# Attention and MLP side by side: projecting the first 512 rows before they are normalised, with dummy products in the opening and new planner thresholds

## The chip, the cores and the metric

The kernel runs on one core of one Trainium2 chip. The metric is the device time of one execution in microseconds (us). TensorE is called PE, VectorE DVE, ScalarE ACT, GpSimd POOL and SyncE SP. A *tile* of x is 128 rows of 640 values; PSUM has eight banks.

## The reference, cut to what matters

S = 2048 rows, D = 640, 32 heads of 20 with one shared key and value head, F = 1536, all bf16.

```python
xn = (x - mean(x)) / sqrt(var(x) + 1e-5)          # per row
q = (xn @ wq) -> 32 heads; k = xn @ wk; v = xn @ wv
p = softmax(q @ k.T * 20 ** -0.5)                 # per head
attn = concat_heads(p @ v) @ wo
h = relu(xn @ w1 + b1) ** 2
return x + attn + (h @ w2 + b2)
```

## The kernel before, in words

**A planner orders everything.** The Python code holds a list scheduler (`Sched`). Streams (generators) ask for pieces of work with `Req(engine, duration, latency, instructions, dependencies, priority)`, and `Until` holds a stream back. When the kernel is built, the planner picks piece after piece with durations written in the code, and so fixes one static instruction order for each engine. On the chip every engine runs its list in order and waits on semaphores for what its pieces depend on. Landing times of DMAs are also figures in the code (`xland`, `TLAND`, `XRL`). If one of them is too short, the chip's engine simply waits at that place of its list.

**Attention.** Queries lie in 4 blocks of 512 rows, times 8 groups of 4 heads: 32 blocks `b` (`NBLK`; block 0 is heads 0 to 3, block 1 heads 4 to 7). Keys come in 16 tiles. A *unit* is one head, one key tile and 512 queries: one score product `ps<-qT,kT` (L1154) into a PSUM bank. There are 2,048 units. 1,468 go to ACT, which takes two or three at once (L1334, 1,024 or 1,536 columns, into a ring `PT`). 580 go to DVE, which makes an approximate exponential from integer arithmetic (L1431 from PSUM into `pbx`, then L1452 and on POOL L1514 for three shifted copies). Value products are L1621. Thresholds that decide how the planner shares the units and when it gives up banks are in `PLAN`, one row for each half block, 64 rows of 13 figures.

**The rest** is put between the units: query projections (`u_QT`, `u_QP`), the MLP's first product (`u_FFN`, L939 on DVE, squares on POOL L947), and the output products (L783). Norms and packed heads travel by small DMAs on SP's queue.

**The opening.** SP loads x in five DMAs (tiles 0-1, 2-3, 4-7, 8-11, 12-15; row `st*128 + p` on partition p) with wq between the third and the fourth; ACT's queue loads wk and wv. `x_sb` lies in `pbx`, normalised tiles `xn_sb` in `big`. Per tile: statistics (`stats`, L683 and L686 on DVE; tile 2 on ACT, L673 and L675), then `rst` (L694 LN and L698 exponential on ACT, one for four tiles), then `xnorm` (L712 on DVE; tile 3 on ACT, L714). Tiles 0 to 4 are transposed by PE (L772) and copied out (L727 on ACT, L726 on DVE); tiles 5 to 15 by transposing DMAs on SP (L732). `u_K0` and `u_Q0` project the first 512 rows, in halves of 256, with `wk_c` and `wq_sb`; the mean key of the first tile is subtracted from all keys (`nk0`, L816, L817, L821). `u_V` makes values (L842, L846, then POOL L850 and L854). `S_PRO` starts these streams for tiles 0 to 3. Key tiles 4 to 7 (`u_KT`, copy at L807) need tiles 4 to 7 transposed.

**Dummy products.** `warmup` (L650) gives PE 20 products of 512 columns on constants. `S_FILL` adds fill products when PE's planned load in the last 1,500 ns is under `PE_FILL`: L1551 before the first value product (4 x 512 columns), L1550 with zeros afterwards.

## Time and profile before

| | |
|---|---|
| median of 3 runs | 702.17 us (701.01 to 703.31) |
| profiled execution | 702.17 us, span 700.0 us |
| mean granted PE clock | 0.995 |
| busy PE / DVE / ACT / POOL | 684.3 / 659.3 / 680.5 / 411.8 us |
| ACT exponentials (L1334) | 672.1 us in 684 instructions |
| first exponential starts | 14.31 us |
| last exponential ends | 691.56 us |

The span runs from the first to the last instruction; the 2.17 us beside it lie outside. Busy PE is modelled and overlaps, so 98% is not PE at its peak. The opening up to 14 us, the exponentials, and 8 us of output products, additions and stores at the end follow one another.

### The profile page before, as it was taken

The numbers are of one execution on the slowest core, as the hardware profiler recorded it, in microseconds if no ns is written. First come the engines' busy times: TensorE is split into PE (matmuls) and PEld (weight loads), VectorE is DVE, ScalarE is ACT, GpSimd is POOL, SyncE is SP. The second block draws the span as 40 slices with busy tenths as digits, with TensorE's granted clock in tenths as the row PEclk, the third lists the DMA queues.
The fourth block names the chain that finished last, engine by engine and source line by source line (L and its number), as shares of the span: only waits on it lengthen the run. The fifth ranks groups of instructions, "written<-read, shape, count | busy, mean of one in ns | idle before, by whom it ended". The sixth has DMA issues, their size and how long they took to land.

```text
span 700.0 us, 23262 instructions
## 1 busy us (share of the span) xinstructions
PE 684.3 (98%) x9837; PEld 218.7 (31%) x9837; DVE 659.3 (94%) x1135; ACT 680.5 (97%) x705; POOL 411.8 (59%) x678
## 2 busy tenths in 40 slices
PE   8899999999999999999999999999999999999997
PEld 4232222222223333332223333333223333333333
DVE  6788999999999999999999999999999999999994
ACT  6799999999999999999999999999999999999995
POOL 2245576767675656667766666666666656656510
PEclk9899999999999999999999999999999999999999
DMA  6433233101110111210110111111110011121001
GB/s 201 67 74 120 54 109 85 27 20 27 29 20 13 39 26 39 50 36 19 24 25 18 45 27 39 32 30 41 28 26 19 15 38 47 27 50 32 11 3 40
DMA packets 37330, 29.30 MB, mean 42 GB/s; under 512 B 19594, under 2 KB 32875, under 8 KB 37227
## 3 DMA queue, kind: packets, MB, share of 16 engines
q1 hardware_dynamic: 35915, 27.76, 16.6%
q8 instruction: 79, 1.29, 0.8%
q10 hardware_dynamic: 1312, 0.05, 0.1%
q14 instruction: 24, 0.20, 0.1%
HBM read 10.87 MB, written 2.62 MB: 19 GB/s over the span
## 4 chain that ended last, share of the span: by engine, by line
ACT 76%; PE 13%; DVE 10%; DMA 1%; issue 0%; POOL 0%; DVEq 0%; POOLq 0%
ACT PT L1334 75%; DVE pbx L1431 5%; PE ps L783 4%; PE ps L1621 4%; PE ps L1154 4%; DVE pbx L1452 3%; PE ps L650 1%; DVE hT_tmp L939 1%; DMA xnT<-big 1%; DVE stats L683 0%; DVE Tn L1666 0%; DVE big L712 0%; ACT xnT L727 0%; DVE qpk L894 0%; PE ps L1551 0%
## 5 line engine op out<-in xcount | busy, mean ns | idle before, releaser
L1334 ACT ACTIVATE PT<-ps 128x1024 bf16<-128x1024 f32 (+1 forms) x684 | 672.1, 1138 | 5.3 <-PE ps L1154 5.0
L1514 POOL TENSOR_SCALAR pbx<-pbx 128x576 int16<-128x576 uint16 (+17 forms) x508 | 309.5, 629 | 185.6 <-DVE pbx L1452 173.8
L1431 DVE TENSOR_SCALAR pbx<-ps 128x512 int16<-128x512 f32 (+1 forms) x568 | 377.2, 689 | 16.6 <-PE ps L1154 15.3
L1154 PE MATMUL ps<-qT,kT 20*128 20x512 bf16 x2048 | 267.9, 385 | 3.8 <-ACT PT L1334 1.9
L1452 DVE TENSOR_SCALAR pbx<-pbx 128x2048 int16<-128x2048 int16 x305 | 209.2, 705 | 0.8
L1621 PE MATMUL ps<-pbx,vp 128*32 128x512 bf16 x1740 | 161.4, 384 | 1.1 <-DVE pbx L1452 0.8
L1154 PEld LDWEIGHTS ps<-qT,kT 20*128 20x128 bf16 x2048 | 66.9, 91 | 260.6 <-ACT PT L1334 183.3
L1621 PE MATMUL ps<-PT,vx 128*32 128x512 bf16 x1468 | 142.2, 384 | 1.8 <-ACT PT L1334 1.8
L783 PE MATMUL ps<-w_sb,big 128*32 128x320 bf16 x1536 | 80.7, 302 | 0.1
L783 PE MATMUL ps<-xnT,w_sb 128*32 128x512 bf16 x960 | 77.3, 384 | 0.4 <-DVE pbx L1431 0.2
L947 POOL TENSOR_TENSOR big<-hT_tmp 128x224 bf16<-128x224 bf16 (+4 forms) x85 | 55.8, 668 | 32.5 <-DVE pbx L1452 32.5
L1621 PEld LDWEIGHTS ps<-pbx,vp 128*32 128x32 bf16 x1740 | 42.9, 95 | 50.0 <-issue 33.8
L1621 PE MATMUL ps<-pbx,vx 128*32 128x512 bf16 x580 | 57.3, 385 | 0.3
L1621 PEld LDWEIGHTS ps<-PT,vx 128*32 128x32 bf16 x1468 | 38.1, 95 | 44.2 <-issue 32.0
L1682 POOL TENSOR_TENSOR OTs<-Tn,Rb 128x224 bf16<-128x224 f32 (+5 forms) x38 | 32.1, 844 | 15.2 <-DVE pbx L1452 13.2
L783 PEld LDWEIGHTS ps<-w_sb,big 128*32 128x32 bf16 x1536 | 30.8, 95 | 31.9 <-issue 25.6
L939 DVE TENSOR_SCALAR hT_tmp<-ps,b1col 128x512 bf16<-128x512 f32 x48 | 35.3, 735 | 1.5 <-PE ps L783 1.5
L783 PE MATMUL ps<-wo_p,OTp 120*32 120x320 bf16 (+1 forms) x640 | 34.4, 302 | 0.2 <-DVE pbx L1431 0.2
L783 PE MATMUL ps<-xnT,wq_sb 128*32 128x512 bf16 (+2 forms) x435 | 33.4, 373 | 0.0
L783 PEld LDWEIGHTS ps<-xnT,w_sb 128*32 128x32 bf16 x960 | 19.1, 94 | 29.1 <-issue 21.4
L1621 PEld LDWEIGHTS ps<-pbx,vx 128*32 128x32 bf16 x580 | 15.2, 95 | 17.8 <-issue 11.8
L1666 DVE COPY Tn<-ps 128x512 f32<-128x512 f32 x29 | 19.7, 679 | 0.1
(75 smaller groups left out, 176.3 us busy)
## 6 DMA issues: line engine op xcount, KB each, us to landing
Rb<-Rr SPq DMA_DIRECT2D x29, 256.0 KB
xres<-in_A_x_dram SPq DMA_DIRECT2D x16, 160.0 KB
out_dram<-out_sb SPq DMA_DIRECT2D x16, 160.0 KB
qT<-qpk SPq DMA_DIRECT2D x105, 20.0 KB
pbx<-in_A_x_dram SPq DMA_DIRECT2D x3, 640.0 KB
w_sb<-in_B_w_dram SPq DMA_DIRECT2D x1, 1920.0 KB
OTp<-OTs SPq DMA_DIRECT2D x96, 20.0 KB
w_sb<-in_B_w_dram SPq DMA_DIRECT2D x4, 480.0 KB
```

The costliest lines, as they stand in the source:

```text
L650: [(lambda e, i=i: e.matmul(ps[:, (2, 4, 5, 6, 7)[i % 5], :], ones_bf[:, :], hT_tmp[:, 0, :], start=True, stop=True)) for i in range(20)]),
L783: return lambda e: e.matmul(ps[32 * j:32 * j + m, b_[0], 0:n], Lj, R, start=first, stop=last, tile_position=(0, 32 * j))
L939: v = yield Req(("dve", 658.0, 742.0, [lambda e: e.tensor_scalar(out=hT_tmp[:, k, :], in0=ps[:, b_[0], :], scalar1=b1col[:, f:f + 1], scal ...
L947: w = yield from pieces(512, 139.0, 1.7, lambda c0, c1: (lambda e: e.tensor_tensor(out=h2T[:, qc % 2, f, c0:c1], in0=hT_tmp[:, k, c0:c1], ...
L1154: ins.append(lambda e, i=i, b=b, t=t, h=h: e.matmul(ps[:, i, :], kT[32 * h:32 * h + DH, t * 128:(t + 1) * 128], qT[32 * h:32 * h + DH, b % ...
L1334: op = yield Req(("act", d_, d_ + 107.0, [lambda e, slot=slot, n=n, src=src: e.activation(out=PT[:, slot:slot + n, :], in_=ps[:, src, :], ...
L1431: return Req(("dve", d_, d_ + 82.0, [lambda e: e.tensor_scalar(out=PB[:, k, hsl, :], in0=ps[:, bk:bk + np_, :], scalar1=OFFS, scalar2=0.0, ...
L1452: return Req(("dve", 600.0, 684.0, [lambda e: e.tensor_scalar(out=PB[:, k, :, :], in0=PB[:, s, :, :], scalar1=PH_D[j], scalar2=None, op0=A ...
L1514: return lambda e: e.tensor_scalar(out=PB[:, k, :, :].rearrange("p h n -> p (h n)")[:, c0:c1], in0=PBU[:, s, :, :].rearrange("p h n -> p ( ...
L1621: ins = [(lambda e, h=h, first=first, last=last: e.matmul(ps[32 * h:32 * h + 32, bk, :], lhs, rhs[h], start=first, stop=last, tile_positio ...
L1666: v = yield Req(("dve", 600.0, 682.0, [lambda e: e.tensor_copy(out=Tn[:, tb, :], in_=ps[:, pvb, :])]), (lambda: None if oldt() is None els ...
L1682: w = yield from pieces(512, 138.0, 2.14, lambda c0, c1: (lambda e: e.tensor_tensor(out=dst[:, c0:c1], in0=Tn[:, tb, c0:c1], in1=Rb[:, a, ...
```

## The change: what it does, and the diff

1. **Raw projection of the first 512 rows.** For tiles 0 to 3, raw x is transposed on PE (`raw`) into `xrT` and multiplied by the weights of blocks 0 and 1, wk and wv only (`wr`, 200 columns, loaded by four extra small DMAs, `wra` and `wrb`). The result has rows on partitions. The mean is taken out inside PSUM: two more products (L758, L759) with a diagonal of means (`dg`) and the weights' negative column sums in two bf16 parts (`colsum`, `cb`). The row's scale is applied while copying out of PSUM (`nat_q`, `nat_v`, `khalf`), then the small results (128x128, padded heads) are transposed (`turn4`). Before, x was normalised first, transposed and then projected by `u_Q0`, `u_K0`, `u_V(0)` and `u_QT(1)`, which go.
2. **Rows.** Partition p of a 512-row block now holds rows 4p to 4p+3, so that the runs in memory of the five x loads are 2,560 or 5,120 B instead of 1,280. Outputs and residual reads follow. wq is loaded after x.
3. **Other normalisations.** All 16 tiles are normalised on POOL, with statistics all on DVE; tiles 0 to 3 come last. Tiles 5, 6 and 7 are transposed by PE, tile 4 and all others by 13 DMAs.
4. **Dummy products.** The warm-up is 20 products of 128 columns. Fills before the first value product are single ones of 256 columns, into banks chosen by the state of the opening.
5. **Figures.** All 64 `PLAN` rows, DMA landing times, thresholds and priorities. When a product needs evenly spaced banks, the planner now also considers later start times. POOL's value scaling gets a second operation, by 1.0.

```diff
 PLAN = [ ... 64 rows replaced ... ]
-PET = (4,)
-SAT = (0.0, 0.0, 18000.0, 28000.0)
+PET = (5, 6, 7)
+SAT = (0.0, 0.0, 16000.0, 26000.0)
+NWARM = 20
+FDUR, FN = 115.0, 256
+PE_FILL0 = 2300.0
+NOFILL = (3200.0, 4600.0)
+TELAND = 4500.0
-PE_FILL2 = 1000.0
+PE_FILL2 = 1500.0
-        xv = A_x[0].rearrange("(st p) d -> p st d", p=128)
+        xv = A_x[0].rearrange("(c p i) d -> p c i d", p=128, i=4)
+        dma("sp", "wra", [lambda e: e.dma_start(wr[:, :, 0:RQ], wqv[:, :, 0:RQ]), lambda e: e.dma_start(wr[:, :, RQ:RK], wkv)], [], RLAND)
+        dma("sp", "wrb", [lambda e: e.dma_start(wr[:, :, RK:R1], wqv[:, :, RQ:2 * RQ]), lambda e: e.dma_start(wr[:, :, R1:RN], wvv)], [], RLAND + 1200.0)
         x_dma(2)
-        dma("sp", "wq", ...)
         x_dma(3)
         x_dma(4)
+        dma("sp", "wq", ...)
+            if st in XPOOL:
+                alts = [("pool", 700.0, 760.0, alts[0][3])]
+        def raw(st):
+            lo = xrT[:, :, 128 * st:128 * st + 128]
+            v = yield Req(("pe", 560.0, 730.0, [... e.transpose(out=psbf(st)[...], in_=x_sb[:, st, dt * 128:(dt + 1) * 128], identity=ident[:]) ...]),
+                          (lambda: get(x_name(st), "ident", "warmup")), 0.1 * st, f"T{st}", ...)
+            v = yield Req(("act", 640.0, 720.0, [lambda e: e.activation(out=lo, in_=psbf(st)[...], func=AF.Identity)]), [v], 1, f"TR{st}")
+            w = yield Req(("dve", 100.0, 170.0, [lambda e: e.tensor_scalar(out=dg[:, st, :], in0=ident[:, :], scalar1=mv[:, st, 0:1], ...)]), ...)
+        def proj(st, k):
+            fix = [lambda e: e.matmul(dst, dg[:, st, :], cb[:, 0, c0:c1], start=False, stop=False),
+                   lambda e: e.matmul(dst, dg[:, st, :], cb[:, 1, c0:c1], start=False, stop=True)]
+        def colsum(k):
+            v = yield Req(("pe", d_, d_ + 165.0, [... e.matmul(ps[:, 7, c0:c1], ones_bf[:, :], wr[:, dt, c0:c1], ...) ...]), ...)
+        def nat_q(st, g, prio):
+            d_ = ("dve", 150.0, 230.0, [lambda e: e.tensor_scalar(out=padded(st, g), in0=src, scalar1=rstd[:, st:st + 1], scalar2=QSCALE, op0=ALU.mult, op1=ALU.mult)])
+            a_ = ("act", 130.0, 210.0, [lambda e: e.activation(out=padded(st, g), in_=src, func=AF.Identity, scale=rq[:, st:st + 1])])
+        def turn4(bk, g, hf, n, deps, prio, name):
+            return Req(("pe", 70.0 * n, ..., [... e.transpose(out=psbf(bk)[...], in_=qn[:, st, g, :], identity=ident[:]) ...]), ...)
-            dma("sp", f"TE{st}", ..., *((4000.0, 2400.0) if ... else (2900.0, 1300.0)))
+            dma("sp", f"TE{st}", ..., *((TELAND + 500.0, 2400.0) if ... else (TELAND, 1300.0)))
+                    for tt in sorted({t} | {f for f in ft if f > t}):
+                        if not na or evenly([x for x in pool if freeat(x) <= tt + plan("await_")], na) is not None:
+                            t = tt
+                            break
+            def early(bk, dd, name="fill"):
+                return Req(("pe", FDUR, FDUR + PELAT, [lambda e: e.matmul(ps[:, bk, 0:FN], ones_bf[:, :], hT_tmp[:, 0, 0:FN], start=True, stop=True)]), ...)
```

## The prediction, made before the changed kernel ran

> **What bounds the kernel now.** I read first the chain that ended last and the costliest groups, then the waits of ScalarE (ACT), then the order of time up to 34 us, then busy time by stretch.

> ```profile
> ACT 76%; PE 13%; DVE 10%; DMA 1%; issue 0%; POOL 0%; DVEq 0%; POOLq 0%
> L1334 ACT ACTIVATE PT<-ps 128x1024 bf16<-128x1024 f32 (+1 forms) x684 | 672.1, 1138 | 5.3 <-PE ps L1154 5.0
> ```

> The waits (times, then the longest), and ACT in order of time:

> ```profile
> ACT PT L1334 <- PE ps L1154: 5.0, 4, 2.5
> ```

> ```profile
> 14.31 1.02 ACT L1334 ACTIVATE PT<-ps 128x1024 bf16<-128x1024 f32 x1 [0.48 <-PE ps L1154]
> ...
> 26.01 1.02 ACT L1334 ACTIVATE PT<-ps 128x1024 bf16<-128x1024 f32 x1 [2.52 <-PE ps L1154]
> ...
> 29.02 1.02 ACT L1334 ACTIVATE PT<-ps 128x1024 bf16<-128x1024 f32 x1 [0.47 <-PE ps L1154]
> ...
> 31.51 1.02 ACT L1334 ACTIVATE PT<-ps 128x1024 bf16<-128x1024 f32 x1 [1.47 <-PE ps L1154]
> 688.64 2.92 ACT L1334 ACTIVATE PT<-ps 128x1536 bf16<-128x1536 f32 x2
> ```

> ACT's exponentials carry three quarters of the chain. In the whole run ACT waits before them only four times, and the first four lines are these waits: 0.48 us before the first, then 2.52, 0.47 and 1.47, all before 31.6 us. So the span of 700.0 is four pieces: 14.31 of opening, 8.44 of tail (691.56 to 700.0), 4.46 of waits between 23 and 32 us, and 672.8 of exponentials back to back. A change to the opening is worth what it takes from the first and third piece, if the fourth stays.

> PE at its stop, and stretches, whose columns after the length are busy time of PE, its weight loads, DVE, ACT and POOL, then granted clock, DMA share and GB/s:

> ```profile
> 24.72 0.71 PE L842 MATMUL ps<-wv_c,xnT 128*128 128x20 bf16 x20 [2.38 <-DMA xnT<-big]
> ```

> ```profile
> 23.00:24.00 1.00, 0.00 (x0) 0.00 (x0) 0.34 (x1) 0.49 (x2) 0.00 (x0) 1.00 0.12 16
> 24.00:25.00 1.00, 0.28 (x10) 0.28 (x11) 0.00 (x0) 0.00 (x0) 0.00 (x0) 0.55 0.00 0
> ...
> 29.00:30.00 1.00, 1.00 (x12) 0.35 (x16) 0.00 (x0) 0.98 (x1) 1.00 (x3) 0.50 0.67 132
> ...
> 31.00:32.00 1.00, 1.00 (x18) 0.27 (x14) 0.16 (x1) 0.49 (x1) 0.86 (x3) 1.00 0.56 111
> ...
> 400.00:500.00 100.00, 99.95 (x1487) 31.77 (x1479) 97.66 (x165) 100.00 (x105) 63.22 (x103) 1.00 0.16 37
> ```

> PE stood from 22.34 to 24.72 for the transposing DMAs of tiles 5 to 7; meanwhile the granted clock fell to 0.5, and it came back only near 31 us. Everything for key tiles 4 to 7 (V, K) lay behind that, and their keys were in place at 30.7. Later nothing waits: ACT 100.00 of 100, DVE 97.66.

> **The change, part by part.** *What does not move.* ACT has 578 exponentials of 1,024 columns and 104 of 1,536 instead of 584 and 100, the same 1,468 units: 4 x 1.50 - 6 x 1.08 = -0.5 us by mean duration, less by pitch; I count 0. Score and value products, DVE's 580 units, the output tiles and the tail's instructions keep their number. Tail 8.4, stream 672.8.

> *The start.* Removed from the path: all four tiles' statistics, ACT's two statistics passes (0.74 and 0.83 plus readouts), LN, RS, four normalisations, and PE's dummies, which ended at 9.70 although the first normalised tiles were there at 8.3. Now raw tiles are transposed on arrival, and LN/RS and small corrections follow the products. In order:

> - x tiles 0 and 1 landed at 3.95 (first DVE statistics), 2 and 3 by 5.02. Their runs in memory double to 2,560 B; the two landings lay 1.07 apart, so half of that is the most to gain: 3.4 to 3.95, I take 3.7.
> - Transposes: 128 columns took 0.107 us in the early dummies (0.43 per 512) and 0.065 later (20 in 1.29). At the slow figure a tile takes 0.54. ACT's first copy begins at 4.45 with 0.2 of handover (ACT's own waits on PE: 0.22, 0.23). Copies are 0.62 each (four in 2.49); the third ends at 6.4. DVE's statistics of tiles 0 and 1 took 3.95 to 6.19, now done by 6.1, hidden.
> - LN 0.2: 6.6. Column sums (5 products of 100 columns, 0.42) run after the fourth transpose, 6.1 to 6.5, if the small weights are there. Their ACT copy 0.2 ends at 6.9, DVE's remainder at 7.3, the four mean corrections for two tiles at 7.7.
> - DVE is inside a statistics step (0.42) and a diagonal (0.17) until 8.0; three scalings of 0.17 give the first half's queries at 8.5. Two transposes and handovers: 8.95; ACT's copy (0.38) ends at 9.5.
> - ACT then does two RS and two query scalings, 0.2 each: 10.3; transposes and handovers 10.9; copy 11.3. From that copy's end to the first exponential was 0.49 (13.82 to 14.31); three score products at the slow clock add 0.2. **First exponential at 12.0, gain 2.3.** The first half's keys (0.47 copy after a correction on DVE) are done near 10.3, hidden, and cost their excess if over 11.3.

> *Dummies.* 20 warm-up products of 128 columns instead of 20 of 512, 21 short ones placed between. Each is 0.1 to 0.2 us ahead of whatever is queued behind it on PE. Most stand where PE waits; three precede a transpose of the chain, so 0 to 0.6. I take 0, because PE is released late there by DVE and ACT.

> On the clock the trace says: dense products from 1.51 became fast at 7.03, and after the stop of 2.4 us the clock was 0.5 from 24.1 to 30.9, twice 3.4 us. I price the opening with slow products throughout. [...]

> *Small weights.* Four DMAs (two of 640 runs of 160 B, two of 640 of 40 B) enter SP's queue behind x tiles 0 to 3 and ahead of tiles 4 to 15; the full wq goes from ahead of tiles 8 to 15 to behind them. No row shows their landing. The queue with only small runs spent 0.1% of 16 engines' span on 1,312 packets, some 9 ns each; the main queue 16.6% on 35,915, 52 ns each. So 80 packets per engine are 0.7 to 4.1 us after x1 at 5.0: the first pair lands at 5.7 to 9.1. I take 6.1, nearest to the small-run row. At 9.1 the column sums end 3.0 later, less the 1.3 that the chain waits for DVE and statistics anyway: first exponential 13.7. The second pair also matters: its column sums stand on PE ahead of the first scores. The full wq is covered: its first product now stands on PE behind 96 score units, where it stood ahead of the first.

> *The waits at 23 to 32 us.* Queries of blocks 0 and 1 with key tiles 0 to 3 are 2 x 4 x 4 = 32 units. ACT's pitch was 21.44/23 = 0.93 per pair, so they last 14.7 plus 0.4 for LN/RS: 12.0 to 27.1. DVE takes none of them now, since its first exponential stands behind the copy of the next keys; before, it had taken four by 23.4. Those next keys: DVE from 10.5 does ten statistics (4.2), four aggregates (0.5), keys' second half and sums (1.2), eight small scalings (1.2): 17.6. Normalisation moves to POOL, 16 instructions. Nearest rows: int16 128x640 0.724, two-input bf16 128x512 1.04, or 1.3 for 640; I take 0.75 (one tensor input, like the first), end 1.3. Four are done at 20.6. Tiles 5 to 7 turn on PE (0.45 and 0.48 of DVE each, done near 22). Tile 4's DMA, issued near 18.4, lands after 2.6 to 7.8 (three took 16.89 to 24.72); I take 5: 23.4. V and K at full clock took 37.92 to 41.97 later in the trace: 4.05. Keys at 27.5, scores 0.5 later. **About 1.0 of waiting is left of 4.46, gain 3.5.** PE, queued behind tile 4's DMA, had 26 units issued by then; ACT has work to 24.5.

> [...]

> *Later.* POOL had 11 idle us before 28.8; its 12 to 21 us of normalisation fill that. DVE loses 15 normalisations (6 us) and gains two statistics and about 25 small steps (4). Before, DVE still had nine statistics and eight normalisations after 32 us, 6 us; now none, which pays for starting its exponentials later. SP has 13 transposes instead of 11, ahead of w1, whose first users are background. Residual reads and output writes keep 1,280 B runs: 0.

> **Sum.** 12.0 + 672.8 + 1.0 + 8.4 = 694.2 against 700.0, so -5.8. The profiled execution took 702.17, the median of the three runs (2.17 outside its span): **696.4**.

> **Rivals.**
> *A, the keys come late again* (POOL 1.3 each, +2.2; DMA 7.8, +2.8): each us after 27.1 is a us, up to all 4.46. Only the start is gained: 699.9. For it, the measured DMA landing; against, only one such DMA is needed.
> *B, small weights late.* At 9.1 and 13.2 the second pair holds the first scores: first exponential near 14.4, only the waits gained: 698.7.
> *C, slower: the new order loses in the steady part.* There are 64 half blocks, each with its own thresholds, and DVE has only 12.7 us idle between 100 and 600. If a bank or ring place comes late at each hand-over, ACT waits. From 0.09 us per half block the gain is gone, from 0.13 it is slower; at 0.13 the time is 704.7. Against: before had no such wait after 32 us, with the same instruction counts.
> *D, the dummies don't hold the clock* (the change not doing what it says): a slow spell at the K step costs 0.47 + 1.47 as before: 698.3.

> **Chances.** Forecast 0.57, A 0.16, B 0.07, C 0.15, D 0.05. Runs differ from 701.0 to 703.3, so about 0.3%, 2.1 us, can be told from none. A lies on that bound and goes half to same; of C 0.13 is slower. Faster 0.57 + 0.08 + 0.07 + 0.05 = 0.77, same 0.08 + 0.02 = 0.10, slower 0.13. Low end: first exponential 11.0, no wait left, 0.9 of scatter: 693.5. High end: through A and B into the beginning of C, 702.5.

> **What would show it.** First exponential near 12 and its waits summing to about 1 before 30 us; PE never standing 2 us for the transposing DMA; the granted clock 1.00 from 24 to 31; statistics of POOL's normalisation at 0.7 to 0.8; stretches after 100 us with ACT at 99.7 or more of 100. Wrong would be ACT waits spread over the half blocks, or the first scores waiting for the small weights.

## The result, and the profile after

The changed kernel took **719.56 us** (median of four runs, 718.0 to 726.09), the kernel before 702.06 beside it: a ratio of 1.027 (95% interval 1.020 to 1.033). The forecast of 696.4 was wrong by 23 us and in its sign. The profiled execution took 719.34 us, with a span of 717.6.

From the page of the changed kernel, in its order: the granted PE clock in 40 slices, the chain that ended last, and the costliest group, ACT's exponentials (L1485, before L1334).

```profile
PEclk9955699999999999999999999999999999999999
PE 67%; DVE 21%; ACT 8%; issue 1%; DMA 1%; POOL 1%; SPq 0%; DVEq 0%
L1485 ACT ACTIVATE PT<-ps 128x1024 bf16<-128x1024 f32 (+1 forms) x682 | 677.2, 1130 | 20.9 <-PE ps L1301 19.6
```

The chain has moved from ACT (76% before) to PE (67%), ACT's idle time before an exponential from 5.3 to 20.9 us, and three slices of 18 us show a reduced clock. The opening came out close to the prediction. ACT in order of time (start, length, in brackets the wait before it):

```profile
11.66 4.62 ACT L1485 ACTIVATE PT<-ps 128x1536 bf16<-128x1536 f32 x4 [0.63 <-PE ps L1301]
...
21.68 1.02 ACT L1485 ACTIVATE PT<-ps 128x1024 bf16<-128x1024 f32 x1 [0.36 <-PE ps L1301]
...
39.15 1.02 ACT L1485 ACTIVATE PT<-ps 128x1024 bf16<-128x1024 f32 x1 [1.12 <-PE ps L1301]
40.67 1.02 ACT L1485 ACTIVATE PT<-ps 128x1024 bf16<-128x1024 f32 x1 [0.50 <-PE ps L1301]
42.17 1.02 ACT L1485 ACTIVATE PT<-ps 128x1024 bf16<-128x1024 f32 x1 [0.48 <-PE ps L1301]
```

The first exponential starts at 11.66, and only 0.36 us is waited after it up to 34 us. From 39 us on, while the spell lasts, ACT waits about half a microsecond or more before most of them. Counting off ACT's instructions, its first 32 score units were done at 27.5 us (before: 34.4), 64 at 47.7 (49.3), 128 at 92.5 (78.7), 1,000 at 496.0 (478.3). So a lead of 6.9 us was there, and a little over 20 us went between 28 and 92 us. Busy time by stretch (PE, its weight loads, DVE, ACT, POOL, then clock, DMA share, GB/s) says where:

```profile
25.00:50.00 25.00, 23.71 (x210) 5.24 (x206) 16.31 (x28) 20.31 (x23) 17.24 (x27) 0.66 0.71 159
50.00:75.00 25.00, 25.00 (x193) 4.82 (x190) 10.40 (x17) 16.41 (x17) 6.96 (x13) 0.50 0.05 12
75.00:100.00 25.00, 25.00 (x274) 5.92 (x272) 20.54 (x35) 21.15 (x22) 12.12 (x21) 0.81 0.20 48
100.00:125.00 25.00, 24.53 (x320) 6.66 (x321) 24.91 (x43) 24.89 (x26) 17.44 (x27) 1.00 0.34 98
```

From 50 to 75 us PE counts as busy all the time and issues 193 products; at full clock from 100 to 125 us it issues 320. In the clock's records the half clock lasts from 33.19 to 84.39 us, 51.2 us; a second slow stretch, from 214.10 us, lasts 3.413 us. 51.2 is 15 times 3.413, and the slow stretch of the kernel before, 24.11 to 30.94, is twice it; a stretch of this length on the grid of these records is called a window below. PE around the fall:

```profile
31.71 0.40 PE L1783 MATMUL ps<-PT,vx 128*32 128x512 bf16 x4
32.31 0.39 PE L1301 MATMUL ps<-qT,kT 20*128 20x512 bf16 x3 [0.19 <-ACT PT L1485]
33.22 0.62 PE L1783 MATMUL ps<-PT,vx 128*32 128x512 bf16 x4 [0.52 <-ACT PT L1485]
33.77 0.61 PE L1301 MATMUL ps<-qT,kT 20*128 20x512 bf16 x3
```

No long stop is there, unlike the 2.4 us before the fall in the kernel before: PE, ahead of ACT, waits for free places in ACT's ring, 0.19 and then 0.52 us. Three scores take 0.39 before and 0.61 after.

The dummies tell the two orders apart at this place. Of the 13 groups of zero products in the kernel before, seven start between 32.3 and 36.8 us; of the 8 in the changed kernel, the seventh starts at 31.03 and the eighth at 191.2. First the kernel before (its first and last of the seven), then the changed one:

```profile
32.29 0.40 PE L1550 MATMUL ps<-kT,zeros 128*32 128x512 bf16 x4
...
36.80 0.39 PE L1550 MATMUL ps<-kT,zeros 128*32 128x512 bf16 x4
```

```profile
31.03 0.39 PE L1700 MATMUL ps<-kT,zeros 128*32 128x512 bf16 x4
```

### The profile page after: what moved, and what is told of

Its sections match the earlier page's. It is cut to its first block, busy times and chain, and to the rows that moved or that the text cites. A ratio compares the mean times of both kernels' runs of the same rounds, so it can differ in the third digit from the quotient of the medians.

```text
span 717.6 us, 23193 instructions
## 1 busy us (share of the span) xinstructions
PE 703.0 (98%) x9792; PEld 222.6 (31%) x9792; DVE 662.6 (92%) x1146; ACT 683.7 (95%) x704; POOL 426.9 (59%) x689
## 3 DMA queue, kind: packets, MB, share of 16 engines
q1 hardware_dynamic: 38475, 28.34, 16.6%
q10 hardware_dynamic: 1312, 0.05, 0.1%
## 4 chain that ended last, share of the span: by engine, by line
PE 67%; DVE 21%; ACT 8%; issue 1%; DMA 1%; POOL 1%; SPq 0%; DVEq 0%
PE ps L1783 25%; PE ps L1301 22%; PE ps L950 20%; DVE pbx L1581 11%; ACT PT L1485 8%; DVE pbx L1602 6%; DVE hT_tmp L1086 2%; DVE Tn L1828 1%; DMA Tn<-in_A_wk_dram 1%; DVE stats L696 1%; POOL big L731 0%; DVE out_sb L1144 0%; DVE qpk L1041 0%; PE ps L987 0%; DVE Rb L806 0%
## 5 line engine op out<-in xcount | busy, mean ns | idle before, releaser
L1485 ACT ACTIVATE PT<-ps 128x1024 bf16<-128x1024 f32 (+1 forms) x682 | 677.2, 1130 | 20.9 <-PE ps L1301 19.6
L1664 POOL TENSOR_SCALAR pbx<-pbx 128x576 int16<-128x576 uint16 (+21 forms) x497 | 311.2, 646 | 194.7 <-DVE pbx L1602 185.8
L1301 PE MATMUL ps<-qT,kT 20*128 20x512 bf16 x2048 | 274.2, 394 | 3.5 <-DVE pbx L1581 1.3
L1602 DVE TENSOR_SCALAR pbx<-pbx 128x2048 int16<-128x2048 int16 x303 | 211.8, 717 | 1.0
L1783 PE MATMUL ps<-PT,vx 128*32 128x512 bf16 x1468 | 146.1, 394 | 1.8 <-ACT PT L1485 1.8
L950 PE MATMUL ps<-xnT,w_sb 128*32 128x512 bf16 x960 | 80.2, 394 | 0.2 <-DVE hT_tmp L1086 0.2
L1094 POOL TENSOR_TENSOR big<-hT_tmp 128x288 bf16<-128x288 bf16 (+5 forms) x88 | 56.5, 652 | 31.3 <-DVE pbx L1602 29.5
L1844 POOL TENSOR_TENSOR OTs<-Tn,Rb 128x288 bf16<-128x288 f32 (+5 forms) x43 | 32.8, 768 | 11.7 <-DVE pbx L1602 11.4
L950 PE MATMUL ps<-xnT,wq_sb 128*32 128x512 bf16 x375 | 32.3, 409 | 0.1
L950 PEld LDWEIGHTS ps<-xnT,w_sb 128*32 128x32 bf16 x960 | 19.3, 95 | 29.3 <-issue 21.2
```

What stands on the lines that cost most here:

```text
L950: return lambda e: e.matmul(ps[32 * j:32 * j + m, b_[0], 0:n], Lj, R, start=first, stop=last, tile_position=(0, 32 * j))
L1094: w = yield from pieces(512, 139.0, 1.7, lambda c0, c1: (lambda e: e.tensor_tensor(out=h2T[:, qc % 2, f, c0:c1], in0=hT_tmp[:, k, c0:c1], ...
L1301: ins.append(lambda e, i=i, b=b, t=t, h=h: e.matmul(ps[:, i, :], kT[32 * h:32 * h + DH, t * 128:(t + 1) * 128], qT[32 * h:32 * h + DH, b % ...
L1485: op = yield Req(("act", d_, d_ + 107.0, [lambda e, slot=slot, n=n, src=src: e.activation(out=PT[:, slot:slot + n, :], in_=ps[:, src, :], ...
L1602: return Req(("dve", 600.0, 684.0, [lambda e: e.tensor_scalar(out=PB[:, k, :, :], in0=PB[:, s, :, :], scalar1=PH_D[j], scalar2=None, op0=A ...
L1664: return lambda e: e.tensor_scalar(out=PB[:, k, :, :].rearrange("p h n -> p (h n)")[:, c0:c1], in0=PBU[:, s, :, :].rearrange("p h n -> p ( ...
```

## The experiments

Five theories run through the expectations. Theory 1: the clock falls when too little of PE's array works in a window of 3.41 us, and a slow PE then keeps it low. Theory 2: the new order is late whatever the clock. Theory 3: the dummies take PE time that ACT then lacks. Theory 4 (in one run): POOL's queue is the root. Theory 5 came later, in place of theory 1's measure: what counts is the share of a window in which at least one product *streams*. "A group" is four zero products of 512 columns side by side on the array's four column strips (L1550 before, L1700 after). Edits are made when instructions are written out, so the planned order stays, except where "planned anew" is said; `op.extra` holds the added dummies. The diffs are excerpts, with "..." where lines are left out. Line numbers shift a little between kernels. The kernel before, run beside each of these on the same chip, took 701.76 us (b_nofill, burst, fill_one, cols80), 702.31 (dense, xn_dve, dense_xn, b_cols128), 701.84 (thin, spread, spread_a) and 701.99 (the other four).

**b_nofill: the kernel before, without its 13 groups.**

```diff
+def pv_fill(op):
+    return op.start > 17000.0
...
-            for f in op.ins:
+            for f in ([] if op.name == 'fill' and pv_fill(op) else op.ins):
```

> The kernel before in its own order, without its 13 groups of zero products (L1550). Theory 1: the windows after 17 us lose 1,000 to 1,500 of activity (3,456 becomes 1,900, the windows after 31 us fall from 4,483 to about 3,000), so the clock falls near 20.7 us and stays at 0.5 for tens of us, as in the changed kernel: 715 to 730 us. Theory 2: the dummies do nothing for the order, so the time is within 2 us of 702. Theory 3: 2 to 4 us faster than 702.

Measured 726.95 us, ratio 1.036 (1.030 to 1.042). Clock, and ACT's waits (total, times, longest):

```profile
PEclk9655599999999999999999999999999999999999
```

```profile
ACT PT L1338 <- PE ps L1158: 22.3, 35, 1.6
```

Taking PE work *away* makes the old kernel slow in the same way: half clock from 18.77 to 29.01 and again from 32.42 to 90.45 us, and ACT waiting 22 us. With its dummies this order had one spell of 6.8 us, so a long spell needs no new order.

**burst: the changed order, 12 groups behind one value product at unit 62.**

```diff
+            now = eng == "pe" and op.name == "PV" and op.extra and left and units >= 60
...
-            for f in op.ins:
+            for f in op.ins + (op.extra * 12 if now else []):
```

> The changed kernel in its own order, with 12 dummy groups in a row behind the first value product after score unit 60, in the middle of the slow spell (near 46 us; 12 groups are 5.1 us at the slow clock). At the slow clock a window holds at most 4,096 of activity, and the spell's windows had 2,700 to 3,330. Theory 1: the full window releases the clock within 7 us of the burst, near 52 us instead of 84; about 15 us of the 20 lost are not lost, the burst costs about 4: 705 to 710 us. Theory 2 and 3: the burst only delays what follows, 722 to 726 us.

Measured 702.05 us, ratio 1.001 (0.999 to 1.003), with 2.76 us of useless products added. In the profile the clock holds from 4.94 to 196.09 us; ACT's longest wait, 2.44, stands right behind the burst. Theory 2 is refuted as the cause of the loss: with the clock held, 17 of the 17.5 us are gone. One of its ten executions fell nevertheless (718.39, mean clock 0.971; it is not in the ratio).

**fill_one: the group behind unit 47 three times.**

```diff
+                nfill[0] += len(op.ins) == HPG
+                op.extra = op.ins and len(op.ins) == HPG and nfill[0] == 7
...
-            for f in op.ins:
+            for f in op.ins * (3 if op.extra else 1):
```

> The changed kernel in its own order on every engine, with one dummy group (four zero products, 512 columns) issued three times instead of once: the one behind score unit 47, at 31.0 us, in the window before the clock fell. Theory 1 (activity): the clock is granted for a window of 3.41 us by how much of the array was worked in the window before. Counting each product's columns by the share of the array's 32x32 blocks it uses, windows with 3,456 kept the fast clock and windows with 3,200, 2,432 and 2,048 lost it; the window 29.8 to 33.2 had 3,200. Two more groups make it 4,224, the clock stays at 1.00 past 33 us, the waits from 33 to 84 us go, and the time falls from 719.6 to 698 to 701. Theory 2 (order): the new order itself runs late from 33 us on (banks, value slots, POOL) and the clock only follows the stalls: time within 2 us of 719.6. Theory 3 (occupied PE): PE is full, so more dummies cost their 0.4 us and more.

Measured 717.04 us; three of four executions were at 716.87 to 720.11, one at 699.75 (mean clock 0.998). The profiled one fell one dip later, at 40.65, and again for 51.2 us. So theory 1's 698 to 701 came in one execution of four. With the dip at 33 us filled, the clock fell at the next one here.

**cols80: the planner's count of a score product put back from 128 to 80 columns, planned anew** (25 groups instead of 8). The change raises this count from 80 to 128; the diff ahead of the prediction doesn't print that line.

```diff
-cols=128.0 * len(au), after=t)
+cols=80.0 * len(au), after=t)
```

> The changed kernel planned with one figure as before: a score unit counts 80 columns in PE's load instead of 128, so the planner places 25 dummy groups instead of 8 (two more at score unit 53, near 32.7 us), and the order later is planned anew. Theory 1: the clock stays at 1.00 from 6 us to the end, the fall at 33 us was made by this one figure, 697 to 702 us. Theory 2: still 715 or more. Theory 3: over 720.

Measured 728.9 us, ratio 1.037 (1.033 to 1.042), half clock from 40.62 to 61.10 and from 85.0 to 95.23. Theory 1's 697 to 702 missed, and the times that theories 2 and 3 gave (715 or more, over 720) came. But the long time again goes with a slow clock: ACT waits 18.8 us. There are more groups, but not where the dips are; and anew planned, ACT got 608 x 2 + 88 x 3 = 1,480 units instead of 1,468.

**dense: the changed order, a group behind most value products from unit 20 to 100** (26 more, 34 in all; the expectation took all 34 for added ones). This diff is against burst.

```diff
-            now = eng == "pe" and op.name == "PV" and op.extra and left and units >= 60
+            now = eng == "pe" and op.name == "PV" and op.extra and 20 <= units < 100
...
-            for f in op.ins + (op.extra * 12 if now else []):
+            for f in op.ins + (op.extra * 1 if now else []):
```

> The changed kernel's order with one group of four zero products of 512 columns behind each value product between score units 20 and 100: 34 groups more, 0.22 us of PE each if the four run side by side as elsewhere in the trace, so 7.5 us of PE spread over some 40 us. Theory 1 (the clock falls where PE's array is too little used in a 3.41 us window, and the slow PE then keeps it low): the windows between 30 and 50 us gain 500 to 900 columns each and stay over 3,450, the clock stays at 1.00, time 699 to 703. Theory 2 (the new order itself is late, whatever the clock): 715 to 722. Theory 3 (the dummies take PE time that ACT then waits for): no spell, but ACT's waits grow from the 4.9 us of the run with twelve groups in one place by up to 7 us: 704 to 709.

Measured 704.27 us (701.56 to 705.73), ratio 1.003 (1.001 to 1.004). In the profile there is no fall before 196 us, with POOL's queue as it was: theory 4, by which it would still fall, is out as the root of the spell. Theory 1's number misses by 1 us; the time lies in theory 3's 704 to 709, which also said no spell, and ACT waits 6.5 us in 15 places instead of burst's 4.9 in 6. So the dummies have a price of their own.

**xn_dve: normalisation back on DVE, planned anew; dense_xn: the same with dense's groups; b_cols128: the kernel before, planned anew with 128 columns for a score product.**

```diff
-XPOOL = tuple(range(16))
+XPOOL = ()
```

> The part of the change that moves the 16 normalisations to POOL is undone (they go to DVE), and the planner orders anew: 27 groups of zero products instead of 8. Theory 1: what decides is the array's use between 29 and 45 us. With 27 groups, most of them between units 30 and 70, there should be no long spell, 699 to 704. A rival, theory 4 (POOL's queue is the root: the normalisations stand ahead of the value scaling that PE waits for, and the dummies are beside the point): also no spell, but then it must hold here for the reason that PE never stands over 1 us for vp; the run dense, which leaves POOL's queue alone, would by theory 4 still fall. Theory 2: the time stays 710 or more.

> Both edits: normalisation back on DVE with its 27 zero groups, and a further group behind each value product from unit 20 to 100. Theory 1: clock 1.00 after the first release in every run, 698 to 703, and no execution over 706. Theory 3 (dummies cost PE time): 2 to 5 us longer than xn_dve.

> The kernel before with one edit of the change alone: the planner counts a score product as 128 columns instead of 80 when it decides whether PE needs a dummy (10 zero groups remain of 13, in other places). Theory 1: fewer dummies lower the array's use; before's lowest sliding window after 31 us held 3,728 columns, so a loss of three groups of 512 columns could bring one window to 3,200, at the edge: 702 if none falls, 712 to 722 if one does. Theory 2: 702, since the order of the change is not in it.

Measured 711.75, 715.42 and 713.11 us. In the first two the clock held as theory 1 said, and its times miss; theory 2's number for xn_dve (710 or more) and theory 3's for dense_xn (2 to 5 us over xn_dve; 3.7 measured) came. The third is met in number, but beyond the 6.8 us that the kernel before has, its profile shows only one slow window, at 153 us. In xn_dve the clock is 1.00 from 6.33 us to the end, and the time is still 9.4 us over the kernel before. ACT's exponentials by shape, in xn_dve:

```profile
L1485 ACT ACTIVATE PT<-ps 128x1024 bf16<-128x1024 f32 x615 | 577.4, 1070 | 1.3 <-PE ps L1301 1.2
L1485 ACT ACTIVATE PT<-ps 128x1536 bf16<-128x1536 f32 x86 | 127.9, 1491 | 3.5 <-PE ps L1301 3.5
```

That is 1,488 units, 20 more than 1,468, at 674/1,468 = 0.46 us each: 9.2 us. By terms, xn_dve's span is 9.5 us over the kernel before: exponentials 682.6 against 672.1 (+10.5), tail 10.6 against 8.4 (+2.1), first exponential -2.3, waits -0.8. So the longer time is in the main ACT's larger share, and not the clock. b_cols128 gave ACT 1,480 and had it wait 9.7 us. The thresholds fit one plan, and another plan shares the units in another way. So these three (and cols80) say nothing clean about the part that they undo.

**thin: burst with twelve single products, all on the first column strip.** About the same PE time, a quarter of the array. This diff too is against burst.

```diff
-            for f in op.ins + (op.extra * 12 if now else []):
+            for f in op.ins + (op.extra * 3 if now else []):
...
-... ps[32 * h:32 * h + 32, pvb, :] ... tile_position=(0, 32 * h)
+... ps[0:32, pvb, :] ... tile_position=(0, 0)
```

> The changed kernel's order with the same place for the dummies as the run burst (behind the first value product after score unit 60), but only twelve products, all on the first 32 columns of the array, so that they run one after another: about 2.6 us of PE as in burst, with a quarter of the array (12 x 512 x 4 of 16 blocks = 1,536 columns of full array instead of 6,144). Theory 1 (what counts is how much of the array works in a 3.41 us window): the window that holds them stays under 3,300, the clock falls near 37 to 41 us in most executions and the time is 714 to 722. Theory 5 (what counts is that PE is not idle): same occupation as burst, so no fall, 701 to 704.

Measured 701.47 us; the ratio of 1.000 (0.998 to 1.002) leaves out the one execution of ten that had the spell (717.17). PE at the dummies:

```profile
37.69 2.32 PE L1798 MATMUL ps<-kT,zeros 128*32 128x512 bf16 x10
```

Ten products one after another took 2.32 us, so (2.32 - 0.39)/9 = 0.214 us per 512 columns. The window from 36.9 us held 0.346 of the array's full work by theory 1's count and did not fall, while windows with 0.39 to 0.44 fell in other runs (0.39 the one before 33.19 us in the changed kernel: 3,200 of 8,192 columns). Theory 1's measure is refuted.

**b_thin: the kernel before, each of its 13 groups cut to the first product.**

```diff
-            for f in op.ins:
+            for f in (op.ins[:1] if op.name == 'fill' and len(op.ins) == 4 and op.start > 17000.0 else op.ins):
```

> The kernel before with its 13 groups of four zero products side by side cut to the first product of each, at the same places: the streaming time of a group stays (512 columns, about 0.21 us), the part of the array that works falls to a quarter. Theory 1 (share of the array): 384 columns of full array less per group, nearly as without dummies, so a long spell from about 32 us in most executions, 715 to 727. Theory 5 (the share of a window in which at least one product streams; falls were seen at 0.19 to 0.48 of a window, none above): same streaming time as before, no spell beyond before's own at 24 to 31 us, 700.5 to 703.

Measured 701.11 us (697.24 to 702.54), ratio 0.9985 (0.9968 to 1.0001): as the kernel before, and 26 us from b_nofill. Here 13 narrow products did what the 52 did. This is the cleanest evidence for theory 5. In its profile the early spell is one window longer than in the kernel before (20.79 to 31.03 us instead of 24.11 to 30.94), behind a window that streamed 0.505.

**spread and spread_a: the changed order, a group behind each set of score products from unit 41 to 62 and 70 to 82; spread also two near 195 us. spread_sig, spread_thin: spread_a with the scores' signal given ahead of the dummy, with groups or with single products. spread_thin_late: spread_thin with two more singles behind each set from unit 514 to 530.** The edit of spread_thin:

```diff
+            n = 41 <= units <= 62 or 70 <= units <= 82
             if op.sig and op.ins:
                 ins.then_inc(op.sem, op.amt)
+            for f in ext[:1] * n if eng == "pe" and op.name == "QK" and ext else []:
+                f(e)
```

> The changed kernel's order, one group of four zero products side by side behind each group of score products between units 41 and 62 and between 70 and 82 (the stretches near 30 to 37 us and 43 to 48 us where a sliding window of 3.41 us held under 3,450 columns in the run burst), and two behind each between units 514 and 530 (near 195 us, where one window fell in burst and dense). Theory 1: no spell after the first release, clock 1.00, ACT's waits about 2 to 3 us instead of 4.9 and 6.5, 698 to 700.5, faster than before. Theory 2 (order late): 715 or more. Theory 3 (dummies cost what they take): 702 to 705.

> As spread, without the groups near 195 us. Theory 1: no spell before 190 us, one or two slow windows near 195 to 204 us, which cost 1 to 2 us: clock 0.995 to 0.998, 699.5 to 702. If the late groups take more than they save, it is faster than spread.

> The changed kernel's order with a single zero product of 512 columns at each place where spread_a had a group of four, and the signal of the score products given before the dummy instead of behind it. Theory 5 (streaming time): as spread_a, no spell before 190 us, and ACT's waits on the dummies (1.3 us in spread_a) gone: 698.5 to 701. Theory 1 (share of the array): a place adds 128 columns of full array instead of 512, the windows from 30 to 37 us stay at 3,200 to 3,400 and most executions fall: 712 to 720.

> As spread_a, with the signal of the score products given before the dummies: ACT no longer waits for them (1.3 us there). Both theories of the clock: no spell before 190 us; 698.5 to 701, so about 1 us under spread_a's 701.08 and faster than the kernel before. If the waits come from PE being late in any case, no difference from spread_a.

> As spread_thin, with two further single products behind each group of score products between units 514 and 530, near 195 us, where one window of some executions fell. Theory 5: the windows there gain up to 2 x 0.21 us per group, some 2 us in all, streaming share from 0.28 to over 0.48 in most phases: clock 1.00 in most executions, 697.5 to 700. Theory 3 (dummies cost the time they take): 1 to 2 us over spread_thin.

| | us | ratio to before |
|---|---|---|
| spread | 702.76 (701.11 to 706.0) | 1.0019 (1.0000 to 1.0038) |
| spread_a | 701.08 (699.17 to 702.38) | 0.9990 (0.9978 to 1.0001) |
| spread_sig | 701.06 (699.14 to 702.59) | 0.9988 (0.9974 to 1.0003) |
| spread_thin | 700.56 (698.8 to 702.61) | 0.9982 (0.9968 to 0.9996) |
| spread_thin_late | 700.79 (699.84 to 704.45) | 0.9984 (0.9966 to 1.0002) |

None of these 53 executions had the long spell. The signal moved ahead bought nothing (spread_sig against spread_a): the waits then name the scores instead of the dummies. spread and spread_sig were expected to be faster than before and are not. spread_thin_late, expected at 697.5 to 700, holds the clock at 1.00 in nine of eleven executions, but costs as much as the late window did (these nine took 699.84 to 701.2, spread_thin's four at 1.00 took 698.8 to 700.0); its other two took 704.4, and the profiled one of them fell earlier, from 21.41 to 35.07 us, behind a stretch where no dummies had been added. spread_thin is the fastest, 1.4 us under the kernel before, on the edge of what can be told. Its stretches, and its exponentials:

```profile
25.00:50.00 25.00, 23.99 (x283) 7.45 (x281) 18.24 (x34) 23.53 (x28) 20.96 (x32) 1.00 0.69 159
50.00:75.00 25.00, 25.00 (x319) 6.67 (x320) 21.84 (x37) 25.00 (x28) 12.37 (x20) 1.00 0.19 47
75.00:100.00 25.00, 24.90 (x325) 6.71 (x323) 25.00 (x42) 25.00 (x27) 17.30 (x27) 1.00 0.27 68
```

```profile
L1494 ACT ACTIVATE PT<-ps 128x1024 bf16<-128x1024 f32 (+1 forms) x682 | 674.2, 1133 | 5.1 <-PE ps L1310 3.9
```

The same order at full clock: PE is called busy just as before (25.00 of 25), yet issues 319 products instead of 193, and ACT is full.

## Why the prediction was wrong, point by point

**The opening: right in size.** First exponential predicted at 12.0, measured 11.66. x landed at 3.81 (3.7 taken), PE's wait for the small weights ended at 6.61 (6.1). The closeness is in part luck: the steps were priced with slow products throughout, while the full clock was granted from 5.88 us on, and the small weights were 0.5 late. Keys of tiles 4 to 7 were in place at 26.6 (27.5), so the 1.0 us of waiting for them did not come; the 0.36 at 21.68 lies ahead of them. PE stood nowhere for a transposing DMA. The clock was 1.00 from 24 to 31 us as said.

**POOL's normalisation: mis-sized.** Taken at 0.75 each and free, "fill" of idle time. In time order on POOL:

```profile
24.32 9.86 POOL L731 TENSOR_SCALAR big<-pbx,rstd,nmr 128x640 bf16<-128x640 bf16 x11
34.27 2.21 POOL L1664 TENSOR_SCALAR pbx<-pbx 128x576 int16<-128x576 uint16 x3
36.47 0.87 POOL L731 TENSOR_SCALAR big<-pbx,rstd,nmr 128x640 bf16<-128x640 bf16 x1
37.42 0.89 POOL L1002 TENSOR_SCALAR vp<-out_sb 128x80 bf16<-128x80 f32 x3
```

Fifteen of the 16 took 0.87 each. One took 1.30: it began at 32.03, while DVE's L1602 ran, which took 1.07 there (0.72 in the mean). Beside DVE's statistics near 18 us they took 0.87, as much as the last one at 36.47, beside which DVE ran nothing, so nothing was lost there. The value scaling for tiles 8 to 11 (`vp`) stands behind the last normalisation. Where the clock held, PE waited for it 0.64 us, and then ACT 0.55. PE in spread_thin:

```profile
39.71 0.61 PE L1792 MATMUL ps<-pbx,vp 128*32 128x512 bf16 x8 [0.64 <-POOL vp L1011]
```

I had named nothing that is queued behind the normalisations; about half a microsecond of waiting was left out.

**"Steady part unchanged" and rival D: the step that failed.** The sum took the clock as fast after 31 us, and D put a price of 0.47 + 1.47 on one further slow spell at the K step. D's mechanism (the dummies don't hold the clock) was right, and it had been given a chance of 0.05; its price was taken from a spell of 6.8 us. This one lasted 51.2 us. By terms, the profiled execution against the sum: first exponential -0.3, exponentials 677.2 instead of 672.8, +4.4 (one that stands alone takes 1.02 us, in an unbroken row the pitch was 0.93), waits 20.3 instead of 1.0, +19.3, tail 8.24 instead of 8.4, -0.2: together +23.2 of the 23.4 between the spans 694.2 and 717.6. I had costed the dummies as PE time to be hidden, read the diff's `PE_FILL2`, and passed over the edit that counts a score as 128 columns. The order of instructions shows 8 groups instead of 13, and the sum never asked what clock that leaves. That the clock fell without the dummies is shown in the kernel before (b_nofill, half clock from 32.42 to 90.45 us), and that it held with added ones in the changed one (spread_thin, 1.00 from 25 to 100 us); which edit of the change thins the windows is not settled, because the two runs that turned this count over were planned anew.

**Why it lasts so long.** For 17 profiled executions I took each 3.413-us window of the clock's grid and, from PE's records, the part of it in which at least one product streams (from its start for 0.214 us per 512 columns, twice that at half clock: in the slow spell of the changed kernel eight value products took 1.04 and four 0.62, so 0.42 more; in spread_thin at full clock 0.61 and 0.40, so 0.21 more). This is an estimate worked out from the traces and not a counter. All 18 windows after which the clock fell had 0.20 to 0.505 (0.459 before 33.19 us and 0.29 before 214.10 in the changed kernel, 0.324 before 24.11 in the kernel before). Of some 3,270 windows after which it stayed fast, later than 9 us and before 685, eight lie between 0.464 and 0.50 and none under 0.464. So in these executions the two kinds overlap between 0.464 and 0.505. At half clock the shares are higher: the 61 slow windows that stayed slow had up to 0.868, and 15 of the 18 releases came after 0.87 to 0.93 (the other three 0.798 to 0.858). In the spell of the changed kernel the windows lie at 0.77 to 0.857, PE "25.00 of 25" from 50 to 75 us by the profile: window after window short of what stood before 15 of the 18 releases. The window before its release streamed 0.856, no more than several before it that stayed slow. So streaming time alone doesn't say when a spell ends, and what ended this one isn't shown.

The window before 33.19 us was not idle: it was 46% streaming, with no wait of PE over 0.52 us and at most 0.69 us between two streaming products.

**C and the steady part.** After 100 us ACT was 99.5 to 99.9 of 100 in four of five stretches (98.44 from 200 to 300, with the slow window at 214 us), so C's loss did not come in the size that would have taken the gain (5.8 us over all half blocks): from unit 128 on, the changed kernel lost 17.8 - 13.8 = 4.0 us in all.

**Where the rest of the gain is.** spread_thin's profile: 12.10 to the first exponential (12.0 predicted), exponentials 674.2 (672.8), waits 4.5 (1.0), tail 8.25 (8.4): a span of 699.2, 5.0 over the sum. Of the 4.5 us of waits, 0.59, 0.55 and 0.17 lie at 38 to 48 us and 0.38, 0.50 and 0.45 around the slow window at 195 to 199 us; the rest is small. The exponentials' other mix of widths I had counted as 0; they took 1.4 more, of which no run shows the reason. So even with the clock held, the order with its dummies was worth 1.3 us (0.3 to 2.2, by the ratio of spread_thin), not 5.8.

## What to carry to other kernels

Before taking a change as free for PE, count for each 3.413-us window how long PE really streams, at the full clock. In these runs the clock fell behind windows with 0.20 to 0.505, and a spell in which the slow PE had no idle time from 50 us on (25.00 of 25) lasted 51.2 us: behind waits of 0.19 and 0.52 us, a little over 20 us were lost. "Busy" in a profile is no measure of this, and neither is a price taken from an earlier, short spell. Of the dummies against it, one narrow product of 512 columns did what four side by side did (b_thin 701.11 us, the kernel before 701.99; spread_thin 700.56, spread_sig 701.06). They belong into the dips: the 25 groups of cols80, planned for other places, left two slow spells and 728.9 us. And where a planner's figures are tuned to one plan, undo a part in the written-out order, not by planning anew.
